# The gate of a mixture of experts, its normalisations and a part of the first expert's second layer planned with the end of the attention, on one Trainium2 core

## The chip, the cores and the metric

The kernel is one program on one core of a Trainium2 chip. The metric is the time of one execution on the device, in microseconds (us). The median of three runs of the kernel before is given; a traced execution gives the rows. Engines: PE is TensorE (matrix products, weights loaded by PEld), DVE is VectorE, ACT is ScalarE, POOL is GpSimd, SP is SyncE, which issues most of the DMAs.

## The reference: what is computed

Three layers, one after the other. First an attention with 2 batches, 8 heads, 576 positions of 64 numbers and a bias on the scores from a small network. Its output, rearranged, is x: 1152 tokens of 512 numbers. Then a mixture of 8 experts in which every expert sees every token, weighted by a gate that is normalised eight times by rows and columns:

```python
logits = x @ w_gate
logits = logits - logits.max()
P = np.exp(logits)
for _ in range(8):
    P /= P.sum(1, keepdims=True) + 1e-09
    P /= P.sum(0, keepdims=True) + 1e-09
    P *= N / E
for e in range(E):
    h = np.maximum(x @ w1[e], 0.0)
    out += P[:, e:e + 1] * (h @ w2[e])
```

(N = 1152, E = 8, hidden size 1024.) Last comes a second mixture of 8 experts in which each token goes to one expert only, picked by its direction against the experts' embeddings.

## The kernel before, in words

**How it is ordered.** All engines' instructions are recorded first, in the order of the program text, and then put in a written-out order for each engine. `Plan` does this: `call` records an instruction with a cost and with what it must follow (`cells` says what two instructions share; a PSUM tile counts as one cell), and `issue` (line 268) makes a list schedule. Its priorities come first from `due` (the recorded order of PE's work, summed up, and for the others when PE needs them) and then from up to 12 rounds of planning backwards and forwards, of which the plan with the shortest modelled end is kept. What `issue` emits is final: on the chip each engine, and SP's and POOL's DMA queues with them, runs its list from the top. `plan.issue()` is called at line 1388 for a first segment and at the end for the rest, so nothing moves across line 1388 on any engine; an engine that is through with its list of the first segment goes on with its list of the second. Between the two the PSUM pool is changed.

**First segment.** `attention` (line 686) walks over nine row tiles and four head pairs. Its PSUM is the pool `pheads`: `scs`, three tiles of two banks for scores and transposes, `pab` and `pO` of one bank each. `finish` writes x in two f16 parts (hi and lo) to `xa`, `x21`, `x22`. Then the weights of the first expert are loaded and split into hi and lo (`load_plain`), and `plain_ups(tb, ...)` (line 934) computes the first layer with ReLU for the token blocks tb = 0 and 1 of three (192 tokens of each batch in each), by `plain`: eight sums of 24 products (128 x 128 by 192) each, in a ring of the two banks `pab` and `pO`. ACT takes each sum out with a ReLU, DVE makes the remainder. The hidden values go to `hcs` (in `r_k`).

**Second segment.** The pool `pbank` has eight tiles of one bank: six are the ring `banks`, two are `mps`, a ring for small things. The program text then goes:
- `directions` (line 1080): loads the embeddings, normalises them (Square on ACT, a chain of small DVE instructions, a product with the inverse norms), four transposes on PE into a bank of `mps`, taken out by DVE. The result is used by the last expert's routing.
- first expert (e = 0): `plain_ups` for block 2 is recorded behind `gate` (line 830: logits of nine tiles of 128 tokens into `mps`, each reduced by DVE; tiles 1, 4 and 7 in two halves; then a maximum over all and the exponent on ACT), eight times `sinkhorn` (line 850: five DVE instructions, a product with ones on PE, five DVE instructions), `keep_gates` (line 863: a transpose and a store of the gates to DRAM by SP) and `plain_downs(0, ...)` (line 952), the second layer of block 0: four sums of 48 products, each taken out by an ACT copy to `acc` (in `nb`). Then `plain_downs` for blocks 1 and 2.
- `split_x` makes sums and differences of quarters of x for the other experts, on DVE, POOL and ACT. From the second expert on a product of block matrices is done with seven products instead of eight (`unit`, `ups` line 970, `downs` line 1002).
- the weights of the next experts: SP loads them into two staging areas (`r_st`, `r_e`), `block_sums` (line 745) forms sums of blocks by accumulating DMAs of POOL and splits each into hi (ACT) and lo (DVE), for w1 in `r_v` and `r_e`, for w2 in `r_bias`. `r_bias` also holds the first expert's weights, until their last use. The first load of the second expert's w1 is SP's next work behind `directions`' loads.
- the gates of an expert are read back from DRAM by SP (`gated`) and multiplied in by DVE; for the first expert this is done at e = 1 over the whole of `acc`.

All matrix products are done as three f16 products (hi by hi, hi by lo, lo by hi). Every instruction is issued through one helper, line 157, so the profile's rows have that line.

Of the kernel before, what the change touches and what calls it, by code (L numbers as in the profile page):

```python
# [14 lines left out]
ACTF = mybir.ActivationFunctionType  # L15
# [307 lines left out]
def attn_moe_moe_kernel(ctx: ExitStack, tc: tile.TileContext, a, out):  # L323
    nc = tc.nc
    vec, act, pe, pool, sp = nc.vector, nc.scalar, nc.tensor, nc.gpsimd, nc.sync
# [14 lines left out]
    vec, act, pe, pool, sp = (plan.engine(e) for e in "vatgs")  # L340
# [30 lines left out]
    def turn_of(ring):  # L371
        i = turns[id(ring)] = turns.get(id(ring), -1) + 1
        return ring[i % len(ring)]
# [61 lines left out]
    scs = [pheads.tile([128, 1024], F32, name=f"sc{i}") for i in range(3)]  # L435
    pab, pO = (pheads.tile([128, 512], F32, name=n) for n in ("pab", "pO"))
# [17 lines left out]
    def tt(eng, out, in0, in1, op=ALU.add):  # L454
        eng.tensor_tensor(out=out, in0=in0, in1=in1, op=op)
# [3 lines left out]
    w1, b1, w2r = wpk[:, 0:1], wpk[:, 1:2], wpk[:, 2:2 + H]  # L459
# [360 lines left out]
    def pieces_of(r):  # L820
        b, m = divmod(r, 3)
        if m == 1:
            return [(0, b * TB + 128, 64, 0), (1, b * TB, 64, 64)]
        return [(m // 2, b * TB + 32 * m, 128, 0)]
# [5 lines left out]
    def gate():  # L830
        for r in range(NT):
            ps = turn_of(mps)[:, 0:2 * E]
            for half, c0, n, p0 in pieces_of(r):
                xh = (xa[:, 0], xa[:, 1]) if half == 0 else (x21, x22)
                small_logits(
                    ps[p0:p0 + n], lambda k: xh[k // 2][:, 0, k % 2, c0:c0 + n],
                    lambda k: xh[k // 2][:, 1, k % 2, c0:c0 + n], wg,
                )
            vec.tensor_reduce(out=lg[:, r], in_=ps.rearrange("p (t e) -> p e t", t=2), axis=AX.X, op=ALU.add)
        vec.tensor_reduce(out=mx[:, 0:1], in_=lg.rearrange("p t e -> p (t e)"), axis=AX.X, op=ALU.max)  # L840
        ps = turn_of(mps)[0:1, 0:128]
        pe.transpose(ps, mx[:, 0:1], ident)
        vec.tensor_reduce(out=gmx, in_=ps, axis=AX.X, op=ALU.max)
        ps = turn_of(mps)[:, 0:1]
        pe.matmul(out=ps, lhsT=ones[0:1, :], rhs=gmx, start=True, stop=True)
        sc = 1.0 / (C_X * C_W)
        vec.tensor_scalar(mx[:, 1:2], ps, -sc, None, ALU.mult)
        act.activation(P, lg, ACTF.Exp, scale=sc, bias=mx[:, 1:2])

    def sinkhorn():  # L850
        vec.tensor_reduce(out=rs, in_=P, axis=AX.X, op=ALU.add)
        vec.tensor_scalar(rs, rs, 1e-9, None, ALU.add)
        vec.reciprocal(rs, rs)
        tt(vec, P, P, rs.unsqueeze(2).to_broadcast([128, NT, E]), ALU.mult)
        ps = turn_of(mps)[:, 0:NT * E].rearrange("p (t e) -> p t e", t=NT)
        pe.matmul(out=ps, lhsT=ones, rhs=P, start=True, stop=True)
        vec.tensor_reduce(out=cs, in_=ps.rearrange("p t e -> p e t"), axis=AX.X, op=ALU.add)
        vec.tensor_scalar(cs, cs, 1e-9, None, ALU.add)
        vec.reciprocal(cs, cs)
        vec.tensor_scalar(cs, cs, N / E, None, ALU.mult)  # L860
        tt(vec, P, P, cs.unsqueeze(1).to_broadcast([128, NT, E]), ALU.mult)

    def keep_gates():

        vec.tensor_copy(lg.rearrange("p t e -> p (t e)").rearrange("p (e t) -> p e t", e=E), P.rearrange("p t e -> p e t"))
        ps = turn_of(mps)[0:E * NT, 0:128]
        pe.transpose(ps, lg.rearrange("p t e -> p (t e)"), ident)
        vec.tensor_copy(pt, ps)
        sp.dma_start(out=gates.rearrange("e (t p) -> (e t) p", p=128), in_=pt)
# [64 lines left out]
    def plain_ups(tb, w, hc, ring):  # L934

        n = slice(tb * TB, tb * TB + TB)
        x = ((xa[:, 0], xa[:, 1]), (x21, x22))
        for f in range(2):
            f2 = slice(2 * f, 2 * f + 2)

            def take(r, g, ps):
                hi, lo = (hc[:, HB0[r][g], i, f2] for i in range(2))
                act.activation(hi, ps, ACTF.Relu)
                vec.scalar_tensor_tensor(out=lo, in0=ps, scalar=0.0, in1=hi, op0=ALU.max, op1=ALU.subtract)

            plain(
                w, lambda r, h, a_, k: x[r][h][:, a_, k, n], 2,
                lambda w, h, g, k, b_, i: w[k][h][:, b_, g, 256 * f + 128 * i:256 * f + 128 * i + 128], take, ring)

    HB0 = ((0, 1), (3, 2))  # L950

    def plain_downs(tb, w, hc):
        sum_ = acc[:, :, tb].rearrange("p d h n -> p h d n")
        plain(
            w, lambda r, h, a_, k: hc[:, HB0[r][h], a_, k], 4,
            lambda w, h, g, k, b_, i: w[k // 2][h][:, b_, k % 2, 256 * g + 128 * i:256 * g + 128 * i + 128],
            lambda r, g, ps: act.activation(sum_[:, r, 2 * g:2 * g + 2], ps, ACTF.Copy), banks)

    def takers(c11, c12, c21, c22, p1):

# [422 lines left out]

    w1, w2 = (load_plain(a[name][0], name == "m1w1") for name in ("m1w1", "m1w2"))
    hb = [(turn_of(hcs), turn_of(hss)) for _ in range(2)]
    for tb in range(2):
        plain_ups(tb, w1, hb[tb][0], [pab, pO])
    plan.issue()
    stack.close()
    pbank = psum_pool("pbank", 1)  # L1390
# [1 line left out]
    mps = [m0, m1]  # L1392
# [3 lines left out]
    for e in range(E):  # L1396
        ring = banks8 if 0 < e < E - 1 else banks
        if e:
            w2 = load_w2(a["m1w2"][e])
        hb = hb[:2 if e == 0 else 0]  # L1400
        for tb in range(3):
            if e or tb > 1:
                hb.append((turn_of(hcs), turn_of(hss)))
            if e:
                ups(tb, w1, *hb[tb], ring, cs4)
            elif tb > 1:
                plain_ups(tb, w1, hb[tb][0], banks)
            if tb == 1:
                if e == 0:
                    gate()  # L1410
                    for it in range(8):
                        sinkhorn()
                    keep_gates()
                    plain_downs(0, w2, hb[0][0])
                    continue
                if e == 1:
                    for i in range(3):
                        sum_ = acc[:, :, i].rearrange("p d h n -> p h d n")
                        gated(0, i, sum_, sum_)
                downs(e, 0, w2, *hb[0], ring)  # L1420
        if e == 0:
            for tb in range(3):
                split_x(tb)
        if e + 1 < E:
            w1 = load_w1(a["m1w1"][e + 1])
        for tb in (1, 2):
            if e == 0:
                plain_downs(tb, w2, hb[tb][0])
            else:
                downs(e, tb, w2, *hb[tb], ring, *([route(tb - 1)] if e == E - 1 else []))  # L1430

# [71 lines left out]
```

## Time and profile before

| | |
|---|---|
| median of 3 runs | 1126.13 us (1124.84 to 1126.91) |
| the profiled execution | 1124.44 us |
| its span, first to last instruction | 1122.5 us |
| mean granted clock of PE in it | 0.973 of full speed |
| PE busy | 1039.4 us (93%), 12043 products |
| DVE busy | 898.7 us (80%), 1519 instructions |
| ACT busy | 639.0 us (57%) |
| POOL busy | 284.8 us (25%) |

Stretches: the attention ends about 233 us after the start of the span, the first segment at 261.3, the first expert at about 338; the seven other experts of the first mixture end about 920, the rest is the second mixture. In the rows a time is us from the start of the span; "x24" is a number of instructions shown as one line; a bracket at the end is the idle time of the engine just before and what ended it. Tiles are named by region, buffer numbers left out: `pb` is the pool `pbank`, `r_k` hidden values, `nb` the sums `acc` and the combinations of x, `r_e` also holds the gate's small tiles.

### The profile page before, as it was taken

Reading aid. Unit: us, or ns where it says so; the run is one execution under the profiler, and the core shown is the slowest. Engines: PE = TensorE matmul, PEld = TensorE weight load, DVE = VectorE, ACT = ScalarE, POOL = GpSimd, SP = SyncE. Lnnn points to the kernel's source line nnn. Section 1 sums busy time; section 2 is a strip of 40 time slices with the busy share of each in tenths; the row PEclk is TensorE's granted clock in tenths of the full one; section 3 lists DMA queues with packets and bytes.
Section 4 is the critical chain, followed back from the end, with each engine's and each line's share of the span. In section 5 each row is a group of like instructions: output and inputs, shape, how many; then the busy total and the mean of one; then the engine's idle time right before and its main releaser. Section 6 shows DMA issues by size and latency. Waiting matters only on the chain. (4 is left out here: it accounts for less than half of the span.)

```text
span 1122.5 us, 28865 instructions
## 1 busy us (share of the span) xinstructions
PE 1039.4 (93%) x12043; PEld 912.6 (81%) x12043; DVE 898.7 (80%) x1519; ACT 639.0 (57%) x930; POOL 284.8 (25%) x233
## 2 busy tenths in 40 slices
PE   6788999997899999999999999999999999879996
PEld 2346665787899999899999899999999999756663
DVE  7896768627858898898898988997987988957982
ACT  6787988833415355454454554553643545648872
POOL 2651000005411122322221412322322211054221
PEclk8899999999899999999999999999999999979998
DMA  9743324122562247347346436536526122247683
GB/s 291 193 142 85 77 64 126 60 95 42 134 136 58 56 119 159 76 102 165 96 102 147 114 79 143 140 84 154 125 56 149 28 83 95 86 85 201 196 275 113
DMA packets 79472, 132.72 MB, mean 118 GB/s; under 512 B 19030, under 2 KB 40222, under 8 KB 79080
## 3 DMA queue, kind: packets, MB, share of 16 engines
q1 hardware_dynamic: 61432, 95.94, 28.1%
q0 software_dynamic: 17904, 34.88, 17.4%
q8 instruction: 96, 1.57, 0.6%
q14 instruction: 40, 0.33, 0.1%
HBM read 111.87 MB, written 5.29 MB: 104 GB/s over the span
## 5 line engine op out<-in xcount | busy, mean ns | idle before, releaser
L157 PEld LDWEIGHTS <-r_bias 128*128 128x128 f16 x4920 | 402.5, 99 | 22.8 <-issue 21.5
L157 PEld LDWEIGHTS <-r_v 128*128 128x128 f16 x2880 | 235.8, 98 | 11.7 <-issue 9.6
L157 PE MATMUL pb<-r_k,r_bias 128*128 128x192 f16 x2448 | 225.9, 248 | 7.9 <-DVE r_e L157 6.1
L157 POOL TENSOR_TENSOR r_q<-r_w,r_q 128x768 f16<-128x768 f32 (+1 forms) x54 | 103.3, 1913 | 260.4 <-ACT r_q L157 258.6
L157 PE MATMUL pb<-nb,r_v 128*128 128x192 f16 x1260 | 150.1, 246 | 0.7 <-DVE r_e L157 0.6
L157 PE MATMUL pb<-r_q,r_bias 128*128 128x192 f16 x1512 | 133.4, 247 | 3.8 <-DVE r_e L157 2.7
L157 PE MATMUL pb<-nb,r_e 128*128 128x192 f16 x756 | 103.6, 246 | 0.0
L157 PEld LDWEIGHTS <-r_e 128*128 128x128 f16 x1137 | 95.3, 98 | 1.1 <-issue 1.1
L157 PE MATMUL pb<-xa,r_v 128*128 128x192 f16 x1008 | 95.4, 246 | 0.0
L157 POOL DMA_DIRECT2D r_st<-r_st x42 | 44.0, 1049 | 185.4 <-DMA r_st<-in_m1w 81.1
L157 PEld LDWEIGHTS <-r_q 128*128 128x128 f16 (+1 forms) x560 | 41.3, 101 | 39.8 <-issue 17.5
L157 DVE CUSTOM_DVE_ANT_0 r_e<-sc,nb 128x576 f32<-128x576 f32 x72 | 53.5, 754 | 22.2 <-PE sc L157 16.2
L157 ACT ACTIVATE r_q<-r_w 128x1152 f16<-128x1152 f32 x50 | 57.9, 1158 | 16.8 <-DVE r_w L157 12.8
L157 ACT ACTIVATE r_e<-r_e,mn 128x576 f32<-128x576 f32 x72 | 55.3, 769 | 16.2 <-DVE mn L157 15.9
L157 ACT ACTIVATE r_bias<-r_bias,r_w 128x576 f32<-128x576 f32 x72 | 59.4, 859 | 8.8 <-PE pab L157 5.7
L157 POOL DMA_DIRECT2D r_e<-r_e x42 | 40.9, 973 | 73.3 <-DVE r_w L157 15.7
L157 DVE TENSOR_TENSOR r_w<-pb,r_k 128x384 f32<-128x384 f32 x96 | 52.9, 551 | 7.9 <-PE pb L157 6.8
L157 ACT ACTIVATE r_bias<-r_st 128x1024 f16<-128x1024 f32 (+1 forms) x45 | 44.0, 984 | 26.6 <-PE pb L157 11.9
L157 PE MATMUL pab<-r_bias,r_w 128*32 128x288 f32 x472 | 46.8, 436 | 13.3 <-DVE r_bias L157 8.3
L157 DVE TENSOR_TENSOR r_e<-pb,r_k 128x384 f32<-128x384 f32 x93 | 51.3, 552 | 8.7 <-PE pb L157 6.7
L157 ACT ACTIVATE r_k<-pb 128x384 f32<-128x384 f32 (+1 forms) x71 | 34.2, 485 | 40.4 <-PE pb L157 35.9
L157 DVE TENSOR_TENSOR r_w<-pb,r_w 128x384 f32<-128x384 f32 x64 | 35.2, 550 | 25.0 <-PE pb L157 24.9
(221 smaller groups left out, 2014.7 us busy)
## 6 DMA issues: line engine op xcount, KB each, us to landing
r_k<-in_m2w SPq DMA_DIRECT2D x48, 512.0 KB
r_st<-in_m2w SPq DMA_DIRECT2D x24, 512.0 KB
r_e<-in_m2w SPq DMA_DIRECT2D x24, 512.0 KB
r_st<-in_m1w SPq DMA_DIRECT2D x22, 512.0 KB
r_st<-in_m1w SPq DMA_DIRECT2D x42, 256.0 KB
r_e<-in_m1w SPq DMA_DIRECT2D x42, 256.0 KB
r_e<-in_m1w SPq DMA_DIRECT2D x14, 512.0 KB
r_st<-r_st POOLq DMA_DIRECT2D x14, 512.0 KB, 5.4
```

Of the source, the lines that this page charges most:

```text
L157: self.add(e, lambda: f(*a, **k), cost, dma, ins, outs, port)
```

## The change

The gate, its eight normalisations and the store of the gates are recorded in the first segment, between the first layers of block 0 and block 1, and the second layer of block 0 behind them. `mps` is there a ring of one bank, half of the score tile `scs[2]`; the ring `banks` has four banks (one of each of the two other score tiles, `pab` and `pO`), for the first layer of block 1 and the second layer of block 0. Block 0's first layer keeps its two banks. In the second segment these steps are gone; `plain_downs` takes its ring as an argument.

```diff
-    def plain_downs(tb, w, hc):
+    def plain_downs(tb, w, hc, ring):
...
-            lambda r, g, ps: act.activation(sum_[:, r, 2 * g:2 * g + 2], ps, ACTF.Copy), banks)
+            lambda r, g, ps: act.activation(sum_[:, r, 2 * g:2 * g + 2], ps, ACTF.Copy), ring)
...
     hb = [(turn_of(hcs), turn_of(hss)) for _ in range(2)]
-    for tb in range(2):
-        plain_ups(tb, w1, hb[tb][0], [pab, pO])
+
+    mps, banks = [scs[2][:, 0:512]], [scs[0][:, 0:512], scs[1][:, 0:512], pab, pO]
+    plain_ups(0, w1, hb[0][0], [pab, pO])
+    gate()
+    for it in range(8):
+        sinkhorn()
+    keep_gates()
+    plain_ups(1, w1, hb[1][0], banks)
+    plain_downs(0, w2, hb[0][0], banks)
     plan.issue()
     stack.close()
     pbank = psum_pool("pbank", 1)
...
             if tb == 1:
                 if e == 0:
-                    gate()
-                    for it in range(8):
-                        sinkhorn()
-                    keep_gates()
-                    plain_downs(0, w2, hb[0][0])
                     continue
...
             if e == 0:
-                plain_downs(tb, w2, hb[tb][0])
+                plain_downs(tb, w2, hb[tb][0], banks)
```

## Rows read from the trace of the kernel before

**Rows 1.** Busy time of each engine in stretches; the first line names the columns.

```profile
core 0: us, PE busy (x) PEld busy (x) DVE busy (x) ACT busy (x) POOL busy (x), PEclk, DMA share, GB/s
233.00:261.30 28.30, 24.90 (x297) 24.31 (x295) 7.53 (x15) 6.99 (x16) 0.00 (x0) 1.00 0.28 94
...
276.30:283.60 7.30, 0.00 (x0) 0.00 (x0) 7.30 (x6) 1.08 (x3) 6.13 (x8) 0.61 0.73 144
283.60:289.30 5.70, 5.70 (x62) 5.48 (x62) 4.72 (x6) 1.81 (x3) 5.70 (x6) 0.60 0.36 59
289.30:338.00 48.70, 48.70 (x599) 48.29 (x597) 31.23 (x100) 17.04 (x30) 8.90 (x9) 1.00 0.59 143
338.00:421.00 83.00, 81.12 (x976) 80.41 (x975) 72.76 (x95) 40.95 (x50) 16.94 (x13) 1.00 0.32 77
421.00:504.00 83.00, 79.50 (x952) 78.41 (x950) 73.56 (x99) 41.46 (x49) 24.44 (x18) 1.00 0.49 113
```

**Rows 2.** Waits, 228 to 300 us: us in total, times, longest.

```profile
PE pb L157 <- DVE r_e L157: 7.4, 1, 7.4
...
PE pO L157 <- DVE r_k L157: 2.2, 3, 0.8
```

**Rows 3.** Timeline of PE about the seam: start, us, instruction.

```profile
261.34 0.34 PE L157 MATMUL pb<-r_e,xa 128*128 128x16 f16 x8 [1.22 <-DVE r_k L157]
...
274.71 0.41 PE L157 MATMUL pb<-r_e 8*128 8x8 f32 x4
...
283.60 0.39 PE L157 MATMUL pb<-r_e,xa 128*64 128x16 f16 x5 [7.38 <-DVE r_e L157]
```

**Rows 4.** Timeline of DVE, 273 to 284 us.

```profile
273.31 1.12 DVE L157 TENSOR_SCALAR r_e<-r_e,es 8x512 f32<-8x512 f32 x1
...
275.88 5.11 DVE L157 TENSOR_TENSOR nb<-r_e,nb 128x384 f16<-128x384 f32 x2
280.92 2.00 DVE L157 SCALAR_TENSOR_TENSOR r_v<-r_e,r_v 128x512 f16<-128x512 f32 x1
...
283.31 0.24 DVE L157 TENSOR_SCALAR r_e<-pb,tau 128x32 f32<-128x32 f32 x1
```

**Rows 5.** Timeline of PE over one normalisation.

```profile
311.05 0.37 PE L157 MATMUL pb<-r_e 128*128 128x72 f32 x2
311.26 2.64 PE L157 MATMUL pb<-r_k,r_bias 128*128 128x192 f16 x30
313.73 0.66 PE L157 MATMUL pb<-r_k,r_w 128*128 128x192 f16 x6
314.23 0.37 PE L157 MATMUL pb<-r_e 128*128 128x72 f32 x2
```

**Rows 6.** Timeline of DVE: last write of x, maximum, first normalisation, one later normalisation.

```profile
233.09 0.43 DVE L157 TENSOR_TENSOR x<-r_e,x 128x256 f16<-128x256 f32 x1 [0.48 <-ACT x L157]
...
291.43 0.22 DVE L157 TENSOR_REDUCE mx<-r_e 128x1 f32<-128x72 f32 x1
...
295.67 0.21 DVE L157 TENSOR_REDUCE r_e<-r_e 128x9 f32<-128x72 f32 x1
...
311.46 0.23 DVE L157 TENSOR_REDUCE r_e<-pb 128x8 f32<-128x72 f32 x1 [0.85 <-PE pb L157]
...
313.36 0.23 DVE L157 TENSOR_TENSOR r_e<-r_e 128x72 f32<-128x72 f32 x1
```

**Rows 7.** Timeline of ACT: the Square of `directions`.

```profile
260.59 0.61 ACT L157 ACTIVATE r_q<-r_e 8x512 f32<-8x512 f32 x1
```

**Rows 8.** Timeline of SP's queue: the first w1 load of the second expert.

```profile
232.64 1.56 SPq L157 DMA_DIRECT2D r_st<-in_m1w  x3
```

**Rows 9.** Timeline of DVE: last splits of the second expert's w1 and w2.

```profile
302.98 1.22 DVE L157 SCALAR_TENSOR_TENSOR r_e<-r_e 128x1024 f16<-128x1024 f32 x1
...
364.17 1.34 DVE L157 SCALAR_TENSOR_TENSOR r_bias<-r_e,r_bias 128x1024 f16<-128x1024 f32 x1
```

**Rows 10.** Timeline of PE: first products of the second expert's two layers.

```profile
337.92 1.15 PE L157 MATMUL pb<-xa,r_v 128*128 128x192 f16 x12
...
365.82 1.15 PE L157 MATMUL pb<-r_k,r_bias 128*128 128x192 f16 x12
```

## The prediction, made before the changed kernel ran

> **What bounds the kernel now.** I read the table of stages first. From the attention's last writes to the first expert's end [rows 1] it shows TensorE (PE) without a pause from 289.3 to 338 us and nearly so through the experts behind it, but with two holes before: 3.40 us idle in 233 to 261.3, and nothing at all from 276.3 to 283.6 us. In 283.6 to 289.3 it is busy all the time, at a granted clock of 0.60, so mostly at the lower of its two levels. The experts are bound by TensorE: 81.12 of 83 us busy where VectorE (DVE) has 72.76. An us saved ahead of 338 us should therefore reach the end, if what the experts need is there that much earlier too.
>
> The list of waits comes next: the largest wait of PE here is one of 7.4 us for DVE writing r_e, the next are three for DVE in the first layer's loop, 2.2 us in all [rows 2]. The timeline says which instruction it is. PE's first product behind the seam, 261.34, is a gate logit that had waited 1.22 us for the last ReLU remainder; 274.71 are the four transposes of `directions`; 283.60 are the logits that waited [rows 3]. The 64-wide form (128\*64) marks a row tile of two halves, so tile 1, 4 or 7. It needs the other bank of `mps`, the one in which `directions` has left its transposes, and that bank is free only when DVE has taken them out (283.31). That copy is queued behind two 384-wide products that took 5.11 us together and a split of 2.00 us [rows 4]. PE ran nothing in between, so the whole second layer of block 0 stood behind one logit. The five tiles of the other bank, from 261.34 on, had gone before without a stop.
>
> **The change, part by part.** *Removed: the shared bank.* In the second segment nothing but `directions` uses `mps` until the last expert. The 7.4 us go [rows 2]. What can be late next is the transposes themselves (below). *Removed with it: the clock's loss.* 5.70 us of work at 0.60 are 3.42 us at full clock, so 2.28 us [rows 1]. Clock and hole are one event: with no such pause the stretch up to the seam stands at 1.00 in the same table.
>
> *The seam.* The second segment now opens with block 2's first layer, on a bank that the last products of the first segment don't use. If memory is handed over bank by bank, the 1.22 us [rows 3] go; if the whole pool must be empty, the wait is that for the last copy of the second layer, about the same. I take half: 0.6 us gained, ends 0 and 1.2.
>
> *Four banks in place of two.* The 3.40 us idle of 233 to 261.3 [rows 1], less the 1.22 of the seam, are 2.2 us [rows 2]. Block 1 gets four banks, and gate products can fill the pauses of block 0, which keeps two. Ends 0 and 2.2; I take 2.2, because filler is ready from the moment x is complete.
>
> *Moved work on PE* is the same work: a 192-wide product costs 82.4 ns (30 of them in 2.47 us from start to start [rows 5]), so the 192 of `plain_downs` cost 15.8 us wherever they stand; the logits and the normalisations' small products move from one full stretch to another. Cost nothing, gain nothing.
>
> *Moved work on VectorE: the chain of the gate.* x is complete at 233.09 + 0.43 [rows 6]. Logits go through one bank now, nine rounds; the first can start once the bank's last scores are read, before that time. I allow 3 us past the last x for them. From the maximum (291.43) to the first normalisation (295.67) it took 4.2 us [rows 6], then come eight rounds. One round's DVE part took 2.13 us (311.46 to the end of the product begun at 313.36), and the pace was 3.18 us from matmul to matmul (311.05 to 314.23 [rows 5]), in which DVE waited 0.85 us for PE [rows 6]. So at most 25.4 us, and the chain ends near 233.5 + 3 + 4.2 + 25.4 + 1.9 = 268 us, the 1.9 for the transpose and its copies. Its cover is PE's own work: 24.90 us left of the first layer [rows 1], 15.8 of the second, some 4.5 of small products, from 233.0 to 278.2. Ten us of margin; DVE is busy only 7.53 us of 28.30 there, and POOL (GpSimd), beside which the 384-wide products of [rows 4] ran long, not at all [rows 1].
>
> *New waits in it.* PE runs a written-out order, and the planner behind it takes a normalisation for faster than it is: its costs and reaches (`cost`, `OWN`, `REACH`) add to about 2.6 us a round against 3.18 measured. Where PE arrives at a round's product too early, all behind it stands. Ends: 0 and 8 x 0.6 = 4.8 us. The measured 2.13 us of DVE with 0.4 of product and two hand-overs is about 2.8, nearer to the plan, so I take 2.0 us.
>
> *Moved past: the queues.* ScalarE gets the four copies of the second layer ahead of all its work of the second segment, and so `directions` begins with its Square after them. Before, Square started at 260.59, 0.75 us ahead of PE's own start of that segment [rows 3, 7]; now it follows the last copy, 0.9 us after PE's end. The transposes come 1.6 us later relative to PE; I take 1.5, ends 0 and the 9.7 us of the old hole with its clock. The Trainium skill, in "PSUM — Partial Sum Buffer", section "Engine vs sequencer instructions", says that the queues of ScalarE, VectorE and GpSimd are strictly first in, first out; by it the term is the full 1.6, without it Square could start when its rows land and the term would be nothing. The trace agrees as far as it goes: the row of Square shows no idle time ahead of it, so ScalarE went to it straight from the work before [rows 7].
>
> *SP.* The gates' store is the last DMA of the first segment now, and every load of the second stands behind it: `emb`, `tau`, and the second expert's first layer, which was issued from 232.64 on, 29 us before the seam [rows 8]. They now wait till 268 (at the latest 278, if the planner puts the chain last). The 2.6 MB of that layer at the 143 GB/s of the next stage [rows 1] need some 18 us: there by 286 to 296. The last split of these weights ran at 302.98 to 304.2, 43 us after the seam [rows 9], with the gate in between on DVE; PE began them at 337.92 [rows 10]. Now PE comes to them at 278.2 + 48 = 326 (192 + 384 products, transposes). Splits that also take 43 us from the landing end at 329 to 339; without the gate, whose rounds hold 17 us of DVE, I expect 315 to 325. I take 0, ends 0 and 20 (rival C).
>
> **The sum.** Gains: 7.4 + 2.3 + 0.6 + 2.2 = 12.5 us. Losses: 2.0 + 1.5 = 3.5. Rounded for the planner's other choices: 9.5 us off. The profiled execution took 1124.44 us (span 1122.5), 0.15% below the median of 1126.13; taken off the median this gives **1116.6 us**. The whole second segment is planned anew, and its experts lose between 1.9 and 3.5 us of PE per 83 [rows 1]; a new plan can move the seven of them by some 4 us in sum, either way.
>
> **Rivals.** *A, the transposes take the hole's place.* PE is stopped at `directions` instead of at the logit, as its chain on DVE is as late as before: the multiplication that feeds them began at 273.31, 12 us after the seam, and ends 0.3 us before they run [rows 3, 4]. For it: any delay on DVE now counts in full. Against it: the delay of 5.11 us fell behind that one, not ahead of it. Price up to 9.7: about 1124.5. *B, the chain goes last.* The planner ranks by latest start, so the normalisations may be pushed to the segment's end. Then PE has no filler for the last rounds, and the 4.8 us of waits plus the tail of a round come in place of 2.0: 1121. *C, the loads come too late: slower.* With the store at 278 and the full 43 us, the first products of the second expert wait 9 us, and its second layer, whose last split began at 364.17 against a use from 365.82 on [rows 9, 10], a further 10 as it is loaded into the same staging memory. 20 us lost against 9.5 gained: 1136. It decides once both waits exceed 9.5 us, so splits later than about 336 us. For it: most of the 29 us of head start is lost. Against it: the plan for this segment assumes all loads to begin at its start, which is nearer the truth now, and VectorE has 17 us less to do.
>
> **How the numbers follow.** Forecast 0.62, its own range 1111 to 1121 (the gains' ends, 3 to 4 us for the plan). A 0.12, B 0.12, C 0.14. A measurement of this kernel can tell about 0.2%, 2.25 us, from no change. Faster than that: nearly all of the forecast, most of B, a third of A: 0.74. Within: half of A, bits of the others: 0.10. Slower: C and the rest of A: 0.16. The range goes from 1110.5 to 1127, which leaves out C and a lucky plan.
>
> **What would show it.** Right: no PE wait over 2 us between 233 and 330; clock at 1.00 throughout; eight small f32 products between first-layer products ahead of the seam, a seam near 278 to 281, the second expert's first products near 327 to 330; the gates' store near 268. Wrong: a wait of PE for DVE at the four transposes (A); the store within 3 us of the seam and pauses of 0.5 us or more at each round (B); PE waiting for splits in r_v, r_e or r_bias after 326 (C); or the second expert 9 us earlier and the time unchanged, which would say that the experts are not bound by TensorE.

## The result, and the profile after

| | before | after |
|---|---|---|
| median of ten runs | 1125.74 us (1122.04 to 1127.39) | 1115.16 us (1110.84 to 1120.93) |
| ratio of the two, 95% interval | | 0.9906 (0.9890 to 0.9923) |
| the profiled execution, its span | 1124.44, 1122.5 us | 1117.25, 1115.4 us |
| mean granted clock of PE | 0.973 | 0.980 |
| PE busy | 1039.4 us (93%) | 1037.5 us (93%) |
| DVE, ACT, POOL busy | 898.7, 639.0, 284.8 us | 901.0, 637.7, 287.8 us |

The kernel is 10.6 us faster by the medians and 7.1 us by the two profiled spans; forecast were 9.5. The predicted direction, time and range hold. The rest asks whether the steps do.

First the table by stages of the changed kernel, to be read against [rows 1]. The seam now stands at 279.3 us, the second expert's first product at 328.63.

```profile
core 0: us, PE busy (x) PEld busy (x) DVE busy (x) ACT busy (x) POOL busy (x), PEclk, DMA share, GB/s
233.00:261.30 28.30, 28.30 (x365) 27.94 (x364) 19.13 (x79) 7.09 (x15) 0.00 (x0) 1.00 0.01 2
233.00:278.60 45.60, 45.60 (x572) 45.17 (x571) 25.40 (x102) 9.05 (x19) 2.76 (x3) 1.00 0.17 57
278.60:328.60 50.00, 48.10 (x582) 47.76 (x580) 39.21 (x59) 23.97 (x43) 29.81 (x26) 1.00 0.54 128
328.60:412.00 83.40, 78.03 (x910) 77.11 (x908) 68.77 (x91) 41.30 (x50) 19.48 (x15) 0.96 0.42 99
412.00:495.00 83.00, 79.49 (x952) 78.39 (x950) 74.59 (x100) 40.59 (x47) 22.25 (x17) 1.00 0.49 113
...
333.80:338.00 4.20, 1.79 (x22) 1.64 (x20) 1.69 (x2) 1.95 (x2) 0.85 (x1) 0.99 1.06 263
338.00:341.00 3.00, 1.62 (x11) 1.34 (x10) 2.70 (x4) 0.54 (x2) 0.86 (x1) 0.50 0.50 100
341.00:345.00 4.00, 4.00 (x29) 3.81 (x28) 1.62 (x4) 1.65 (x2) 0.78 (x1) 0.54 0.90 292
```

The stretch of the old hole is gone: PE is busy for all 45.60 us up to the seam, at the full clock. DVE does the gate there with 25.40 us of work in 45.60, and POOL beside it next to nothing. But in the stretch of the second expert PE, which was idle for 1.88 us of 83 before, is idle for 5.37 of 83.40 now, and the clock falls to its lower level for some 7 us behind a pause at 334 to 336.

The waits from 228 to 300 us, against [rows 2]: the 7.4 us for r_e and the 2.2 us for r_k are gone. In the whole stretch PE waits twice, 1.3 and 0.6 us, and DVE waits for PE's small products eleven times instead.

```profile
DVE r_e L157 <- PE sc L157: 10.2, 11, 1.7
DVE es L157 <- ACT r_q L157: 8.8, 1, 8.8
...
PE pb L157 <- DVE r_e L157: 1.3, 1, 1.3
PE pb L157 <- ACT nb L157: 0.6, 1, 0.6
```

PE's timeline names the instructions, against [rows 3, 10]: the last normalisation's product and the transposed gates without a pause, the seam, the four transposes of `directions`, and then two waits in the second expert that have no row before.

```profile
266.33 0.37 PE L157 MATMUL sc<-r_e 128*128 128x72 f32 x2
...
268.51 0.27 PE L157 MATMUL sc<-r_e 128*72 128x128 f32 x1
...
279.26 4.12 PE L157 MATMUL pb<-xa,r_bias 128*128 128x192 f16 x48 [0.58 <-ACT nb L157]
...
295.10 0.41 PE L157 MATMUL pb<-r_e 8*128 8x8 f32 x4 [1.32 <-DVE r_e L157]
...
328.63 1.15 PE L157 MATMUL pb<-xa,r_v 128*128 128x192 f16 x12
...
336.65 0.41 PE L157 MATMUL pb<-x,r_v 128*128 128x192 f16 x3 [2.41 <-DVE r_w L157]
...
339.94 2.08 PE L157 MATMUL pb<-nb,r_v 128*128 128x192 f16 x12 [1.38 <-DVE r_w L157]
```

DVE's timeline says what it did ahead of these two waits: its `r_w<-pb`, which takes a sum out of PSUM for PE, stands behind a split of w2 into `r_bias`, and that split waits for ACT's half of it.

```profile
266.74 0.23 DVE L157 TENSOR_REDUCE r_e<-sc 128x8 f32<-128x72 f32 x1 [1.69 <-PE sc L157]
...
279.85 0.32 DVE L157 TENSOR_SCALAR es<-es 8x1 int32<-8x1 int32 x2 [8.76 <-ACT r_q L157]
...
316.17 1.23 DVE L157 SCALAR_TENSOR_TENSOR r_e<-r_e 128x1024 f16<-128x1024 f32 x1 [1.17 <-ACT r_e L157]
...
334.90 1.23 DVE L157 SCALAR_TENSOR_TENSOR r_bias<-r_e,r_bias 128x1024 f16<-128x1024 f32 x1 [3.06 <-ACT r_bias L157]
336.04 0.55 DVE L157 TENSOR_TENSOR r_w<-pb,r_k 128x384 f32<-128x384 f32 x1
338.20 1.23 DVE L157 SCALAR_TENSOR_TENSOR r_bias<-r_st,r_bias 128x1024 f16<-128x1024 f32 x1 [1.60 <-ACT r_bias L157]
339.34 0.55 DVE L157 TENSOR_TENSOR r_w<-pb,r_w 128x384 f32<-128x384 f32 x1
```

ACT's timeline: the Square of `directions` directly behind the last copy of the second layer, and later its halves of w2's splits, which waited for a DMA from SBUF to SBUF, an accumulating one.

```profile
278.72 0.49 ACT L157 ACTIVATE nb<-pO 128x384 f32<-128x384 f32 x1 [3.47 <-PE pO L157]
279.11 0.61 ACT L157 ACTIVATE r_q<-r_e 8x512 f32<-8x512 f32 x1
...
333.81 1.06 ACT L157 ACTIVATE r_bias<-r_e 128x1024 f16<-128x1024 f32 x1 [3.50 <-DMA r_e<-r_e]
...
337.11 1.06 ACT L157 ACTIVATE r_bias<-r_st 128x1024 f16<-128x1024 f32 x1 [2.24 <-DMA r_st<-r_st]
```

SP's queue: the gates' store, and at once behind it the loads that stood at 232.64 before [rows 8].

```profile
269.14 0.35 SPq L157 DMA_DIRECT2D gates<-r_e  x1
269.56 0.28 SPq L157 DMA_DIRECT2D r_e<-in_emb  x1
269.93 1.98 SPq L157 DMA_DIRECT2D r_st<-in_m1w  x3
```

To compare kernels stage by stage I read five marks from each timeline: **A**, PE's first product of the first layer (`pab<-xa,r_bias`); **S**, its first product of the second segment (the first into `pb`); **E**, the second expert's first product (`pb<-xa,r_v`); **G**, SP's read of the third expert's gates; **M**, SP's first load for the second mixture. Distances in us; the last two columns are the start of the first layer and what is left behind M.

| kernel | A to S | S to E | E to G | A to G | G to M | A | behind M |
|---|---|---|---|---|---|---|---|
| before | 67.3 | 76.6 | 49.3 | 193.1 | 531.5 | 194.1 | 203.8 |
| after | 84.4 | 49.4 | 53.2 | 187.0 | 531.6 | 194.9 | 202.0 |
| after_again | 84.6 | 49.4 | 52.2 | 186.2 | 531.7 | 196.9 | 203.2 |
| x2_directions_behind_gate | 67.1 | 77.9 | 47.7 | 192.7 | 533.5 | 196.7 | 201.0 |
| x3_gate_alone | 72.3 | 70.6 | 47.0 | 189.9 | 535.7 | 196.9 | 203.3 |
| x4_two_banks | 86.1 | 49.4 | 51.1 | 186.5 | 531.3 | 196.5 | 203.3 |
| x5_directions_later | 84.6 | 48.0 | 55.8 | 188.3 | 531.3 | 194.6 | 204.7 |
| x7_store_only | 84.6 | 49.7 | 48.2 | 182.5 | 528.7 | 197.3 | 206.1 |
| x7_again | 84.6 | 49.7 | 48.2 | 182.5 | 530.6 | 197.6 | 204.2 |
| x8_store_and_directions | 84.4 | 48.0 | 53.5 | 185.9 | 531.3 | 195.9 | 204.0 |
| x9_own_stage | 84.5 | 52.1 | 48.0 | 184.6 | 532.6 | 195.6 | 201.9 |
| x10_no_sums | 84.3 | 49.4 | 47.3 | 181.1 | 529.4 | 197.4 | 204.3 |
| x12_split_on_vector | 67.3 | 69.4 | 45.9 | 182.6 | 532.9 | 197.4 | 207.6 |

From A to E the change gains 10.1 us (143.8 to 133.8); from E to G it gives 3.9 back; the stretch from G to M takes the same time; 1.8 less is spent behind M and 0.8 more ahead of A. Together 7.1, the difference of the spans.

E is a sharp mark in time, but not in work. In the kernel before, four groups of six products of the first expert still come behind it (`pb<-r_k,r_bias` and `pb<-r_k,r_w` at 339.90, 340.39, 346.83 and 347.32 us). So PE runs 24 products more from E to G than in the changed kernel; first the line of before, then that of after:

```profile
337.92:387.20 49.28, 47.82 (x574) 47.25 (x573) 41.53 (x56) 22.44 (x27) 10.11 (x7) 1.00 0.24 58
```

```profile
328.63:381.83 53.20, 48.25 (x550) 47.48 (x549) 41.15 (x56) 23.36 (x27) 12.66 (x9) 0.94 0.43 101
```

At the 82.4 ns of [rows 5] these 24 products are 2.0 us. For the same work the gain up to the end of the first expert is thus 12.1 us, and the second expert gives 5.9 of it back. Of these, 3.5 are idle time of PE (4.95 us against 1.46) and 2.4 are longer products at the lower clock. Experiment 1 has the same 24 products behind E, experiments 3 and 10 have 12 (1.0 us), the other kernels of the table none.

The changed kernel's two traces agree within 0.2 us up to E and within 1 us up to G, while A and the stretch behind M wander by some 3.5 and 6.5 us over these kernels, though no edit is meant for them. So the distances judge an edit better than a median does.

### The profile page after: what moved, and what is told of

Same layout as the page of the kernel before. It is cut to its first block, busy times and chain, and to the rows that moved or that the text cites. A ratio compares the mean times of both kernels' runs of the same rounds, so it can differ in the third digit from the quotient of the medians.

```text
span 1115.4 us, 28876 instructions
## 1 busy us (share of the span) xinstructions
PE 1037.5 (93%) x12043; PEld 913.4 (82%) x12043; DVE 901.0 (81%) x1519; ACT 637.7 (57%) x930; POOL 287.8 (26%) x233
## 5 line engine op out<-in xcount | busy, mean ns | idle before, releaser
L157 PE MATMUL pb<-r_k,r_bias 128*128 128x192 f16 x2304 | 209.4, 247 | 8.2 <-DVE r_e L157 6.0
L157 DVE SCALAR_TENSOR_TENSOR r_bias<-r_st,r_bias 128x1024 f16<-128x1024 f32 (+1 forms) x45 | 51.8, 1154 | 9.9 <-ACT r_bias L157 9.8
L157 ACT ACTIVATE r_e<-pb 128x384 f32<-128x384 f32 (+1 forms) x34 | 18.0, 530 | 67.2 <-PE pb L157 63.7
```

Of the source, the lines that this page charges most:

```text
L157: self.add(e, lambda: f(*a, **k), cost, dma, ins, outs, port)
```

## The experiments

The theory after the result had three parts: the hole came from the bank that `directions` and the logits shared; the second layer of block 0, put ahead of the seam, covers the end of the gate's chain; and the second expert loses its 3.9 us because the store holds back SP's loads. The rivals: a DVE that is late in any case, whatever bank; filler that doesn't matter; and transposes or a chain of DMAs that are late in spite of early loads.

**1. The shared bank, in the kernel before.** `directions()` is recorded behind the gate, so that nothing stands in a bank of `mps` ahead of the logits.

```diff
-    directions()
...
                     keep_gates()
+                    directions()
```

> The kernel before with one edit: directions is recorded behind the store of the gates instead of ahead of the gate, so the logits need no bank that its transposes hold. The gate stays in the second segment. Theory (the hole was the shared bank): the PE wait of 7.4 us for DVE r_e at 283 us and the stretch at clock 0.60 go, nothing else changes, the loads of the second expert stay as early as before; the time falls by 8 to 10 us, to about 1116, ratio 0.991 to 0.993. Rival (the hole was VectorE's load beside POOL, whatever the bank): another logit or the transposes wait in its place, PE is idle for 4 us or more between 275 and 300, and the time falls by less than 3 us, ratio above 0.997.

1124.64 us against 1127.56, ratio 0.9978 (0.9959 to 0.9996). The one wait is gone, and PE's timeline has four in its place, 6.8 us together, in products of the gate's own chain whose inputs DVE had not yet written; the transposes of `directions` come behind all of them, at 323.42:

```profile
275.71 0.27 PE L157 MATMUL pb<-r_e,mx 128*1 128x128 f32 x1 [1.40 <-DVE es L157]
...
278.65 0.38 PE L157 MATMUL pb<-gmx,r_e 1*128 1x1 f32 x2 [0.69 <-DVE gmx L157]
...
285.36 0.44 PE L157 MATMUL pb<-r_e 128*128 128x72 f32 x2 [2.27 <-DVE es L157]
...
301.24 0.44 PE L157 MATMUL pb<-r_e 128*128 128x72 f32 x2 [2.48 <-DVE r_e L157]
```

S to E is 77.9 us, no shorter than before. The first part of the theory falls: the bank was the place where DVE's lateness showed, not its cause.

**2. POOL off the combinations of x, in the kernel before.** If DVE is late, why? [Rows 4] has two 384-wide subtractions (the prediction calls them products) in 5.11 us while POOL worked. Here all of POOL's additions and subtractions in `split_x` are DVE's: more work for DVE, nothing beside it.

```diff
-        for i, (eng, x) in enumerate(((vec, xa[:, 0]), (pool, xa[:, 1]), (vec, x22), (pool, x21))):
+        for i, (eng, x) in enumerate(((vec, xa[:, 0]), (vec, xa[:, 1]), (vec, x22), (vec, x21))):
...
-        sums(c, t, (pool, vec, pool, vec))
+        sums(c, t, (vec, vec, vec, vec))
...
-            tt((vec, pool)[i % 2], xs[:, i, 1, :, n], src, xs[:, i, 0, :, n], ALU.subtract)
+            tt(vec, xs[:, i, 1, :, n], src, xs[:, i, 0, :, n], ALU.subtract)
```

> The kernel before, with the twelve additions and remainders of split_x that POOL does on VectorE. Theory (the hole at 276 us comes from VectorE's two-input instructions lying beside POOL's): no VectorE instruction of 384 columns over 0.8 us between 262 and 295, the two that took 5.11 us near 1.1, the hole of 7.4 us falls below 4 us although VectorE has 18 instructions more. Rival (the length of VectorE's queue alone makes the hole): it stays above 7 us or grows.

1122.31 us in one run, against 1128.21. The stretch 262 to 289 us by engine, first of the kernel before, then of this one:

```profile
262.00:289.00 27.00, 19.62 (x254) 18.92 (x252) 24.23 (x46) 9.20 (x16) 23.30 (x22) 0.81 0.38 69
```

```profile
262.00:289.00 27.00, 25.78 (x371) 24.89 (x368) 25.11 (x72) 13.93 (x26) 3.46 (x4) 1.00 0.43 99
```

And DVE's subtractions of that form there, by groups of lines (x count, busy us, mean ns), in the same order:

```profile
L157 DVE TENSOR_TENSOR nb<-r_e,nb 128x384 f16<-128x384 f32 x4 | 6.8, 1726 | 0.0
```

```profile
L157 DVE TENSOR_TENSOR nb<-r_e,nb 128x384 f16<-128x384 f32 x6 | 3.2, 539 | 0.0
```

DVE runs 72 instructions in the busy time of 46; the same form takes 539 ns instead of 1726. PE has no wait from the seam to E but the 1.22 us of the seam, the clock stays at 1.00, and S to E falls by 7.2 us (9.2 for the same work), without any move of the gate. That is the main cause of the hole: DVE's instructions stretched beside POOL's, in front of an in-order PE. It isn't all of it, as the edit had the segment planned anew too: DVE's copy starts 0.64 us behind the start of the transposes here (280.04 and 280.68), 8.60 us before [rows 3, 4]. Without the stretching, the two subtractions and the split of [rows 4] would have taken 5.4 us less (5.11 less twice 0.54, 2.00 less the 0.67 of that form in this run; an estimate); the other 2 of the 7.4 us have other reasons, DVE's order among them. The planner knows that the two engines hinder each other, but reckons little for it: it keeps the second of such a pair back for 0.3 of the first one's cost (`LOCK`, lines 58 and 248 to 252). A to G is 10.5 us shorter than before and 4.4 shorter than after; in this one run the stretch behind M is 3.8 us longer than before.

**3. Is the second layer needed as cover?** The changed kernel with `plain_downs` of block 0 back in the second segment:

```diff
-    plain_downs(0, w2, hb[0][0], banks)
     plan.issue()
...
                 if e == 0:
+                    plain_downs(0, w2, hb[0][0], banks)
                     continue
```

> The changed kernel, but the second layer of block 0 stays in the second segment: only the gate, its normalisations and the store are moved. Theory (the second layer covers the end of the chain): PE is out of first-layer work near 262 us while the chain needs till 268, so PE waits in the last two or three normalisations, 4 to 6 us, and the gain over before shrinks to 3 to 6 us, ratio 0.994 to 0.997. Rival (the chain needs no cover, as PE's list goes on in the second segment): PE idle under 2 us between 255 and 275, the time that of the changed kernel, ratio 0.990 to 0.992.

1123.44 us, ratio 0.9963 (0.9949 to 0.9978). PE's timeline about its seam at 269.22:

```profile
266.60 0.44 PE L157 MATMUL sc<-r_e 128*128 128x72 f32 x2 [1.91 <-DVE r_e L157]
268.54 0.30 PE L157 MATMUL sc<-r_e 128*72 128x128 f32 x1 [1.50 <-DVE r_e L157]
269.22 4.30 PE L157 MATMUL pb<-r_k,r_bias 128*128 128x192 f16 x30 [0.38 <-DVE r_e L157]
...
287.01 0.59 PE L157 MATMUL pb<-r_e 8*128 8x8 f32 x4 [3.09 <-DVE r_e L157]
```

The chain's last two steps, the product of the last round and the transposed gates, lie open (3.4 us), and so do the transposes of `directions` (3.1). The row of 30 products behind the pause is 4.30 us long where that of [rows 5] is 2.64: the clock is at 0.60 from 269.22 to 273.5, mostly the lower level. A to E is 142.9 us; most of the gain up to E, 9.1 of 10.1 us (10.1 of 12.1 for the same work), hangs on the cover. This part of the theory holds.

**4. Four banks or two.** Ring `[pab, pO]` in the first segment:

```diff
-    mps, banks = [scs[2][:, 0:512]], [scs[0][:, 0:512], scs[1][:, 0:512], pab, pO]
+    mps, banks = [scs[2][:, 0:512]], [pab, pO]
```

> The changed kernel with two banks, pab and pO, in place of four for the first layer of block 1 and the second layer of block 0. Theory (the four banks took away the pauses of 0.7 us of the first layer): PE waits for DVE or ACT at pO come back, 1.5 to 3 us in all between 233 and the seam, and the seam comes that much later, ratio to before 0.992 to 0.996. Rival (the gate's products fill the pauses, the banks do nothing): PE idle under 0.5 us in that stretch, ratio as for the changed kernel.

1122.29 us, ratio 0.9961 (0.9943 to 0.9980). A to S is 1.6 us longer, though the list of waits has a single new one of 0.25 us there; from E to G 1.1 to 2.1 us come back, and A to G is 186.5, as with four banks. The banks are worth some 1.6 us at the seam and nothing at G, which neither theory had; how, with hardly a wait more in the list, isn't shown. The median is higher than the first one of after by 7 us, the profiled distances are not.

**5. The changed kernel again**, unedited, in a later set.

> The changed kernel once more, unedited, for a second profile beside the others on the same chip: its ten runs spread over 10 us (1110.8 to 1120.9) where those of before spread over 5. Theory (the waits behind the late loads differ from run to run with the DMAs): the second expert loses another amount here than the 3.9 us of the first profile, by 1 us or more, while the rest keeps its distance to before. Rival (the spread comes from the last layer, whose loads follow the routing): the second expert loses the same within 0.5 us and the difference lies behind 950 us.

1120.5 us, ratio 0.9939 (0.9916 to 0.9962), the gain 7 us in place of 10.6. The second expert lost 1.0 us less, the first layer began 2.1 us later (A), and 1.2 more was spent behind M. Both theories hold in part: the loss differs by 1 us, and the rest of the spread lies ahead of A and behind M. The size of the gain is thus known to some 3 us only. The two waits in the second expert's first layer are there again, now 2.35 and 0.56 us.

**6. The store in the second segment.** `keep_gates()`, the transpose with it, recorded behind the seam:

```diff
         sinkhorn()
-    keep_gates()
     plain_ups(1, w1, hb[1][0], banks)
...
                 if e == 0:
+                    keep_gates()
                     continue
```

> The changed kernel with one edit: the transpose and the store of the gates are recorded in the second segment, behind the first layer of block 2, so no DMA of SP waits for the normalisations and the loads of the second expert can start as early as in the kernel before (232 us against 270). Theory (the waits of 2.4 and 1.4 us at 334 to 340 us, with the half clock behind them, come from these late loads): no PE wait over 1 us between 325 and 360, clock 1.00 there, the time 3 to 5 us below the changed kernel, near 1111, ratio to before about 0.987. Rival (VectorE's backlog of the second segment causes them): the waits stay within 1 us of their sum of 3.8 us and the time is that of the changed kernel, ratio 0.990 to 0.992.

1116.89 us, ratio 0.9899 (0.9872 to 0.9926). Loads from 238.47 on, no wait of PE over 0.3 us in the second expert, E to G 45.6 us. But the first segment was planned anew by it: the first layer begins at 208.54, 11 to 14 us later than in the other kernels, so it isn't in the table, the seam stands at 284.89, and the transposes waited longer:

```profile
304.58 0.59 PE L157 MATMUL pb<-r_e 8*128 8x8 f32 x4 [5.57 <-DVE r_e L157]
```

Too much moved at once to be a verdict on the loads.

**7. The store alone.** A stand-in for the store with the same cost keeps the first segment's order; only the DMA itself is issued in the second.

```diff
         vec.tensor_copy(pt, ps)
+        to = gates.rearrange("e (t p) -> (e t) p", p=128)
+        plan.add("s", lambda: None, plan.DMA_ISSUE, to.nbytes() / 360.0 + 10, [pt], [to])
+
+    def store_gates():
...
                 if e == 0:
+                    store_gates()
                     continue
```

> The changed kernel with the store of the gates alone in the second segment; the first segment keeps its order on PE word for word, only SP is not held by the store. Theory (late loads make the waits of the second expert): loads from about 235 us, no PE wait for DVE r_w over 1 us between 325 and 360, and from the second expert's first product to SP's read of the third expert's gates 46 to 48 us where the two profiles of the changed kernel have 53.2 and 52.2. But the splits that are ready earlier stand ahead of the chain of directions on VectorE, so the four transposes wait longer than the 1.3 us, 3 to 6 us, and the time stays within 2 us of the changed kernel, ratio to before 0.990 to 0.994. Rival (nothing stands ahead of that chain): transposes wait under 2 us, the time 4 us lower, ratio under 0.990.

> The changed kernel with the store of the gates alone in the second segment, once more, beside the staging variant on the same chip. Theory (it is truly 3 to 4 us below the changed kernel up to the third expert): first product of the first layer to the third expert's gates 182 to 184 us again (187.0 and 186.2 in the changed kernel), ratio to before 0.988 to 0.991. Rival (the first profile was a lucky one): 185 us or more, ratio above 0.991.

1115.86 us, ratio 0.9898 (0.9876 to 0.9919), and again 1116.21, ratio 0.9889 (0.9856 to 0.9922). The loads start near 236 us, 34 earlier than after. The second expert gets back 4 to 5 us: E to G 48.2 both times. The transposes wait 1.6 us, not longer as was to be feared. The first of its two waits in the second expert:

```profile
338.07 0.41 PE L157 MATMUL pb<-x,r_v 128*128 128x192 f16 x3 [0.90 <-DVE r_w L157]
```

A to G is 182.5 us, 10.6 below before. Of the kernels that leave nothing out it is the best up to M; by the medians it is below after's second set and level with the first.

**8. `directions` later.** In the changed kernel, behind the last block of the first expert; then the same together with the store of 7.

```diff
-    directions()
...
                 plain_downs(tb, w2, hb[tb][0], banks)
+                if tb == 2:
+                    directions()
```

> The changed kernel, directions recorded behind the first expert, its four transposes 804 instructions of PE later; the store stays in the first segment. Theory: the wait of 1.3 us goes and nothing takes its place ahead of the second expert, so its first product stands 1 to 2 us nearer to the seam (50.0 us in the changed kernel); the loads are as late as before, so the waits in the second expert stay or grow by as much, 3 to 5 us: the time within 1.5 us of the changed kernel. Rival (the transposes are what delays VectorE's splits): the waits of the second expert shrink by 2 us or more, the time falls by 3 us or more.

> Both edits together: store in the second segment with the first segment's order kept, directions behind the first expert. Theory (the two waits are tied to VectorE's queue, one by what stands ahead of the transposes, the other by late loads): no PE wait over 1 us between 262 and 360, first product of the second expert 48 to 49 us behind the seam, third expert's gates read 46 to 48 us after that; 4 to 6 us below the changed kernel, ratio to before 0.985 to 0.988, the best of all. Rival (either wait only moves on to the next product that needs VectorE): PE still loses 3 us or more in that stretch and the ratio stays above 0.989.

1121.59 us, ratio 0.9947 (0.9927 to 0.9968), and with the store 1118.84, ratio 0.9922 (0.9897 to 0.9947). S to E is 1.4 us shorter in both, just the wait of the transposes. But the second expert grows to 55.8 and 53.5 us. PE's waits in the second kernel, whose loads began at 234.25:

```profile
331.33 0.41 PE L157 MATMUL pb<-nb,r_v 128*128 128x192 f16 x3 [0.94 <-DVE r_e L157]
...
333.46 0.41 PE L157 MATMUL pb<-nb,r_v 128*128 128x192 f16 x3 [0.98 <-DVE r_w L157]
...
338.47 0.41 PE L157 MATMUL pb<-x,r_v 128*128 128x192 f16 x3 [2.87 <-DVE r_w L157]
```

The longest of them has the pattern of after: DVE's split of w2 at 336.72 had waited 3.31 us for ACT's half, and the sum that PE needed (`r_w<-pb`) stood right behind it at 337.86. So early loads are not enough: what counts is when w2 is through, and where its splits stand in DVE's list.

**9. The accumulating DMAs of w2.** The changed kernel without the three accumulating DMAs for the second expert's w2; it leaves out the sums of blocks of that expert's second layer.

```diff
-            block_sums(w, k, t, lambda x: x)
+            block_sums(w, k, t, lambda x: x, sums)
...
-            w2 = load_w2(a["m1w2"][e])
+            w2 = load_w2(a["m1w2"][e], e != 1)
```

> The changed kernel without the three accumulating DMAs of the second expert's w2 (in each of its two halves): the sums of blocks are left out, the splits run on what was loaded. Every load is as late as in the changed kernel. Theory (not the loads of w1 but the chain of w2, staged behind w1 and summed by three DMAs in a row, holds VectorE's splits and so the products' takers at 334 to 340 us): no PE wait over 1 us between the second expert's first product and 30 us behind it, and from that product to SP's read of the third expert's gates 45 to 48 us (53.2 and 52.2 in the changed kernel). Rival (VectorE simply has too much queued): that distance stays above 50 us.

1113.85 us in one run, against 1128.21. The loads are as late as after's (from 272.33 on), yet PE is busy 19.67 of the 19.92 us behind E:

```profile
331.08:351.00 19.92, 19.67 (x240) 19.52 (x238) 17.22 (x26) 9.51 (x12) 4.53 (x3) 1.00 0.53 131
```

E to G is 47.3 us, 5.9 less than after and just what the kernel before needs for the same work (49.3 less 2.0). The chain of w2 was what the second expert lost its time to. In the changed kernel one of its accumulating DMAs, issued between 326 and 331 us, took 7.0 us to land (the issues of that stretch: KB, then us to landing):

```profile
r_e<-r_e POOLq DMA_DIRECT2D x1, 512.0 KB, 7.0
```

The plan reckons 150 bytes a ns for these (line 144), 3.5 us for 512 KB, and 2.85 us for start and hand-over (lines 57, 201 and 257), 6.4 in all against the 7.0 measured. Why it puts the split of w2 ahead of `r_w<-pb` in DVE's list isn't shown. PE first uses w2 at 361.05, 26 us after that split, so the split could have stood behind the sum; that order was not tried.

**10. A staging place of its own.** The kernel of 7, with the first half of the second expert's w2 loaded into memory that w1 doesn't use (the output of `directions`' Square, which lay there, moves on by 4096):

```diff
-            t = turn_of(stage)
+            t = own if own is not None and k == 0 else turn_of(stage)
...
-            w2 = load_w2(a["m1w2"][e])
+            w2 = load_w2(a["m1w2"][e], at(r_q, 0, [5, 512], F32) if e == 1 else None)
```

> The kernel with the store in the second segment, and the first half of the second expert's w2 staged in memory of its own (the q region, free since the attention's end), so that its load does not wait for the splits of w1 and the second half takes the staging area that w1 leaves first. Theory (the chain of w2 behind w1 in the staging memory bounds the second expert): no PE wait over 0.8 us in the 30 us behind its first product, that product to the third expert's gates 45 to 47 us, 1.5 to 3 us below the kernel with the store moved alone; ratio to before 0.985 to 0.989. Rival (PE is already at its own pace there): no difference beyond 1 us, ratio 0.989 to 0.991.

1118.7 us, ratio 0.9920 (0.9889 to 0.9951). No wait of PE over 0.6 us in the second expert. E to G is 48.0 as in 7, but 12 products of the first expert are in it; for the same work it is 47.0, 1.2 less than in 7, at the edge of what the theory had. The transposes wait 1.75 us longer, with the clock at 0.59 behind them (297.94 to 301), and A to G is 184.6 against 182.5. In the end no gain.

```profile
297.94 0.41 PE L157 MATMUL pb<-r_e 8*128 8x8 f32 x4 [3.39 <-DVE r_e L157]
```

## Why the prediction was right, and which steps were not

**The hole and its clock (7.4 + 2.3): right in amount, the cause only half.** The step "Removed: the shared bank" said that the wait goes because nothing else uses `mps`. It goes, but by experiment 1 a kernel in which the logits don't stand behind that bank keeps nearly all of it elsewhere, and by experiment 2 one in which POOL is kept away from DVE is rid of it with the gate in its old place; some 5.4 of the 7.4 us were stretching. What the change does is to move the gate to a stretch where POOL is idle (no work of it in 233 to 261.3 us). The prediction had this row in hand, [rows 4], and took it for margin, not for the cause.

**The seam (0.6): right in size, by luck.** 1.22 became 0.58. The prediction took the half between two cases; what came is the second, the wait for the last copy of the second layer, and it was only shorter than thought. **Four banks (2.2): the sign right, the size 1.6 us** at the seam, and nothing is left of it at G (experiment 4).

**The chain on DVE: right.** The transposed gates run at 268.51, forecast 268; the seam stands at 279.26, forecast 278.2; the store at 269.14. Its rounds took 3.6 us (seven from 241.15 to 266.33) where at most 3.18 were reckoned; the earlier start of the first of them, 239.84 in place of 240.7, gives only a part of that back, and ten us of margin took in the rest. **Waits in the normalisations (2.0): too dear,** PE waits in none of them; DVE waits for PE in most rounds, up to 1.7 us. That margin was needed: in experiment 3, without it, 3.4 us lie open. Rival B (0.12) didn't come about for that reason.

**The transposes (1.5): right,** 1.32. ACT goes from the last copy at 278.72 to the Square at 279.11, and DVE stands 8.76 us for it. The Trainium skill's "PSUM — Partial Sum Buffer", section "Engine vs sequencer instructions", has these queues strictly first in, first out, and the two rows agree. Rival A (0.12) stayed at this size, and experiment 8 shows it isn't worth removing.

The terms as measured, 7.4 + 2.3 + 0.6 + 2.2 less 1.3, make 11.2 us up to E; 12.1 are there for the same work. The 0.9 between are left open.

**"I take 0" for the loads behind the store: the step that failed.** Rows of w1 came as said: last split at 316.17, forecast 315 to 325, and no product waited for it. But the step looked at w1 and let w2 be, of which only rival C spoke, with its second layer late by 10 us. What came lies between: w2 is in time for its own products, and its splits stand in DVE's list ahead of sums that PE waits for. The price is 3.9 us by the marks and 5.9 for the same work: the waits of 2.41 and 1.38 us and the clock at 0.50 to 0.54 over some 7 us behind them. All the signs that the prediction named for "right" came true, as its window for waits over 2 us ended at 330 and its sign for C was a wait for the splits themselves. Experiment 9 shows the chain of w2 to be the cause, experiment 7 that early loads buy most of it back.

**The total.** A to G gains 6.2 us where 9.5 were forecast; the first set of runs moved by 10.6, the second by 7. So the total agrees better than its steps, and that is luck: the terms up to E came to 2.6 us more than the 9.5, the second expert lost 5.9 where 0 was taken, and the start of the first layer and the stretch behind M cover the difference by their own spread. The listed terms sum to 9.0, not 9.5 (12.5 less 3.5); for the half us added "for the planner's other choices" no row stands. The 4 us by which a new plan was said to move the seven experts came in the second one alone; from G to M 0.1 moved. (Rival C's 9 us fit products that begin at 330; from the 326 of the same prediction and splits at 339 they would be 13.)

**Open.** The changed kernel with `split_x` on DVE alone, which by experiments 2 and 7 could gain on both, was not tried. Nor is it explained why A and the time behind M wander. DVE writes the first part of x at 71.49 us before, 72.86 after and 75.47 in the second run of experiment 7, and A follows 122.0 to 122.6 us later in each, so the wander ahead of A arises in the first 75 us.

## What to carry to other kernels

A wait is named after the place where it shows: before pricing its removal, look whether the engine that is waited for runs its own instructions longer than elsewhere, and beside whom. A serial chain is best put where it has both filler for the engine that it stops and no neighbour that stretches it. When work moves ahead of a queue of loads, follow the loads to the last user, the second weight as well as the first: a piece that is in time for its own product can still stand in an in-order list ahead of something that is due at once.

## What the runs showed of the hardware

- A 384-wide subtraction of two tiles in SBUF on DVE took 1726 ns in the mean beside POOL's additions and 539 ns without them (experiment 2). The Trainium skill, "SBUF — State Buffer", section "Who interferes with whom", says that a DVE instruction with two inputs in SBUF contends with a POOL instruction that reads SBUF; the direction agrees, a size for this case it doesn't give.
- A pause of 2.41 us of PE, soon followed by one of 1.38, was followed by a granted clock of 0.50 to 0.54, the lower level, for about 7 us; the wait of 1.32 us at 295.10 and that of 0.58 us at the seam were not (1.00 over 278.6 to 328.6). The length of the last wait alone does not decide it: behind one of 2.87 us the clock was 1.00 in experiment 8 (338.47 to 341), behind one of 2.65 us 0.58 in experiment 8's first kernel (331.93 to 333.8).
- An accumulating DMA of 512 KB took 7.0 us to land while loads ran beside it; the median of such issues over the whole changed kernel is 5.6 us:

```profile
r_st<-r_st POOLq DMA_DIRECT2D x14, 512.0 KB, 5.6
```
